# Three edits to a gated attention and feed-forward kernel: the engine that copies one weight chunk, the place of one score, and the order of the last gate and up tiles

## The chip, the cores and the metric

The kernel runs on one core of a Trainium2 chip. The metric is the device time of one execution in microseconds (us), taken as the median of repeated runs. Before the change it is 1260.15 us over three runs, which lie between 1259.91 and 1260.15 us.

Five engines of the core work side by side, each through its own instructions in order, and meet at semaphores. TensorE (PE; its weight loads are a row of their own, PEld) multiplies matrices into PSUM. VectorE (DVE) and ScalarE (ACT) do elementwise work and empty PSUM. GpSimd (POOL) does elementwise work on SBUF and issues some DMAs. SyncE (SP) issues the other DMAs.

## The reference

All inputs are float32. There are 2048 tokens of width 448, 16 heads of width 28, and a hidden width of 1792.

```python
def reference(A_x, A_wqkv, A_wo, B_x, B_W_gate, B_W_up, B_W_down, gate_w):
    x = A_x
    g = sigmoid((x * gate_w).sum(-1, keepdims=True))
    # a: attention with 16 heads
    q, k, v = split(x @ wqkv)
    p = softmax(q @ k.T * 28 ** -0.5)
    a = (p @ v) @ wo
    # b: gated feed-forward
    gate = x @ W_gate
    gate = gate * (gate > 0)
    b = (gate * (x @ W_up)) @ W_down
    return g * a + (1 - g) * b
```

## The kernel before

**Split numbers.** Matmuls run on rounded float32 (`F32R`). To keep the precision, an operand is held as a high part (a copy rounded to `F32R`) and a low part (the value minus its high part). A product of two split operands is a list of eleven matmuls (`TERMS`, L68), ordered by the chunk of 128 rows that they need (`BY_CHUNK`, L71). `act_high` (L129) makes a high part on ACT, `dve_high` (L132) on DVE; `low` (L135) makes a low part on DVE, `pool_low` (L138) on POOL. Chunks 0, 1 and 2 of a weight have low parts of their own (places 3, 4, 5); the fourth chunk has 64 rows, which stand twice in place 6, the upper half as high parts and the lower half as low parts.

**Opening.** `split_first` (L270) splits the first group of 224 weight columns, chunk by chunk (`weights(c)`), and the first 512 tokens (`tokens(c)`), in four groups: weights 0 with tokens 0, weights 1 with tokens 1, weights 2 with weights 3, tokens 2 with tokens 3. In `weights(c)` ACT makes every high part; DVE makes the low part of chunk 0, POOL those of chunks 1, 2 and 3. In `tokens(c)` ACT makes the high and DVE the low part. The first projection, `qk(0, 0, BY_CHUNK)` (L415, matmuls at L352), follows the chunks as they come.

**Rounds.** Projections of queries, keys and values follow, with scores and row maxima mixed in. Then a list of rounds (`ROUNDS`, L63) runs the attention and, beside it, 50 of the 56 gate and up tiles. The order of a round is written out by hand as a string, one letter for each TensorE step: `s` one score matmul (L217), whose exponential ACT takes (L219) out of PSUM banks 0 and 1 in turn; `S` the same in another bank; `m` a row-maximum matmul (L191); `x` one gate or up matmul (L526); `l` sends the last projection to DRAM (an ACT and a DVE instruction and a POOL DMA); `u`, `U`, `h` handle the tiles' splits and ends. `FIRST` (L48) is the first round.

**The end.** From L817 on, the kernel works through a list `todo`. `done` is 50, so gate and up tiles 50 to 55 are left. `gate_up(i)` (L754) first issues the split of tile i+1 (`split_f`, L502: three ACT copies, then DVE low parts: two of 128x384 and two of 64x128, tile `wg`, two buffers) and the fetch of tile i+3 (SP), then 22 matmuls of its own tile, then `relu` (ACT) and `spill_h` (L544): DVE multiplies into `h`, and a POOL DMA writes `h` to DRAM. `down(i)` (L802) is 12 matmuls (L789) with the hidden tile `hh` and the down weights `WD`. Ahead of each `down(i)` the loop at L845 issues `fetch_d(i + 4)` (SP DMAs of `wdr` and `hr`) and `split_d(i + 2)` (L776): DVE copies the high part of `WD`, POOL makes its low part, ACT and DVE split `hh`. `split_wo(c)` (L709) does the same for chunk c of the output weights (a DVE copy into `WO`, then a POOL low part). `normalise(15)` (L584) scales the last head on DVE and writes it with four POOL DMAs. `fetch_o(0)` (L718) reads it back with three SP DMAs into the buffer that the raw output weights had. `split_o(0, c)` (L725) splits it in two halves: ACT high parts, POOL low parts of 128x1024 (tile `on`). `wout(0, 0)` (L739) is the first tile of the output projection: 11 matmuls (L744), of which the first seven read high parts and the last four read low parts of chunks 0, 1, 2, 3. Chunks 2 and 3 are in the second half.

Before the change the list runs: tile 50, tile 51, down 0, tile 52, down 1, tile 53, down 2, tile 54, down 3, tile 55, down 4, `wout(0, 0)`, down 5. The `split_wo` steps stand ahead of down 0, tile 52, down 1 and tile 53, `normalise(15)` ahead of down 1, `fetch_o(0)` ahead of down 2, and both halves of `split_o(0)` ahead of tile 55.

Of the kernel before, what the change touches and what calls it, by code (L numbers as in the profile page):

```python
# [26 lines left out]
NF = F // P  # L27
NB = 4
# [16 lines left out]

FIRST = ("ssssssssssssssssmmmmssuxxxxsxmlxsxsxmSxsxsxmSxsxUsxmxsxsxmxsxsxmxsxsxmxsxsxmxsxsxmxsxsxmxsxsxmxsxsxm"  # L48
         "xsxhh")

ONE = ("mSxMxsmSmsxxsMxmsmSxsMxmsmxsMSxsmsmxSMsxmsmSMsxmsxmSMssxmSmxsMsmxNsmxxsMmsxxsmxMxxmsmxsxMsmxsxmMsxms"
# [10 lines left out]

ROUNDS = [(FIRST, 4)] + [(TWO, 4), (THREE, 4), (ONE, 4)] * 7 + [(LATE, 6), (FINAL, 6)]  # L63
NP = 11
# [14 lines left out]
def gated_mix_kernel(ctx, tc, x, wq, wo, wgu, wd, out):  # L79
# [49 lines left out]
    def act_high(dst, src):  # L129
        nc.scalar.activation(dst, src, AF.Copy)  # L130
# [4 lines left out]
    def low(dst, src, high):  # L135
        nc.vector.tensor_tensor(dst, src, f32(high), op=OP.subtract)  # L136
# [99 lines left out]
    with tc.tile_pool(name="qkv", bufs=1) as pa:  # L236
# [33 lines left out]
        def split_first(wr, xr):  # L270

            r = wr.rearrange("p c (a j d) -> p c a j d", a=2, j=4)
            w = W[:, :, :2 * GD].rearrange("p c (j a d) -> p c a j d", a=2, j=4)

            def weights(c):
                act_high(w[:, c if c < 3 else 6], r[:, c])
                yield

                take = pool_low if c else low
                if c < 3:  # L280
                    take(w[:, 3 + c], r[:, c], w[:, c])
                else:
                    take(w[64:, 6], r[64:, 3], w[64:, 6])
                yield

            def tokens(c):
                part = xr[c // 2][2][:, c % 2:c % 2 + 1]
                act_high(X[0][0][:, c:c + 1], part)
                yield
                low(X[0][1][:, c:c + 1], part, X[0][0][:, c:c + 1])  # L290
                yield

            for group in ((weights(0), tokens(0)), (weights(1), tokens(1)), (weights(2), weights(3)),
                          (tokens(2), tokens(3))):
                for _ in range(2):
                    for part in group:
                        next(part)
# [194 lines left out]
    done = sum(n for _, n in ROUNDS) // 2  # L492
# [125 lines left out]
    for r, (order, nu) in enumerate(ROUNDS):  # L618
        ni = order.lower().count("s") // NB
        late = order in (LATE, FINAL)  # L620
        todo = list(range(nxt, nxt + nu))
# [10 lines left out]
        for o in order:  # L632
            if o in "sS":
                i, j = i0 + ns // NB, ns % NB
# [14 lines left out]
            elif o == "x":  # L649
                i, half, k = passes.pop(0)  # L650
# [3 lines left out]
                if k == NT - 1:  # L654
                    i, half, ps = units.pop()
# [161 lines left out]
    todo = [(gate_up, done), (row_sums, H - 1), (gate_up, done + 1)]  # L817
    for i in range(NB * NF):
        todo.append((down, i))
        if done + 2 + i < NB * NF:  # L820
            todo.append((gate_up, done + 2 + i))

    def before(i, *new):
        n = todo.index((down, i))
# [66 lines left out]
```

## Time and profile before

| | |
|---|---|
| median of 3 runs | 1260.15 us (1259.91 to 1260.15) |
| time of the profiled execution | 1259.94 us |
| its span, first to last instruction | 1258.2 us |
| TensorE matmul busy | 1252.8 us, 6687 matmuls |
| VectorE busy | 854.8 us, 1363 instructions |
| ScalarE busy | 748.4 us, 1424 instructions |
| GpSimd busy | 374.3 us, 569 instructions |
| granted TensorE clock, mean over the span | 1.0 |

A timeline row gives the start in us, the length in us, the engine, the line of the kernel, the operation, the tiles as written<-read, their shapes, and how many instructions in a row were merged into it. In square brackets stands the idle time of the engine ahead of the row and what ended it. Instructions of one engine overlap a little at their ends. The matmuls' lengths are modelled: they are pipelined, so the distance from one matmul's start to the next is the better measure, and that is what the text uses. The 1.74 us by which the profiled execution's time exceeds its span lie outside the first and last instruction.

### The profile page before, as it was taken

The page shows a single profiled execution, that of the slowest core. Times are in us where ns is not written, and L with a number is a line of the kernel's source. Part 1 is how long each engine was busy: PE and PEld are TensorE (multiplying, and loading weights), DVE is VectorE, ACT ScalarE, POOL GpSimd, SP SyncE. Part 2 cuts the span into 40 slices and gives each one's busy share as a digit, 9 for nine tenths or more (in the row PEclk, how much of TensorE's full clock was granted, in tenths as well). Part 3 has the DMA queues.
Part 4 walks back from the last instruction along what each step waited for, and adds up shares of the span by engine and source line. Part 5 has one row for each costly group of instructions (what it writes and reads, how often), then busy time and mean ns, then how long its engine had stood idle before and what let it go on. Part 6 is the DMA issues. An engine that isn't in the chain of part 4 may idle for free.

```text
span 1258.2 us, 18270 instructions
## 1 busy us (share of the span) xinstructions
PE 1252.8 (100%) x6687; PEld 919.1 (73%) x6687; DVE 854.8 (68%) x1363; ACT 748.4 (59%) x1424; POOL 374.3 (30%) x569
## 2 busy tenths in 40 slices
PE   9999999999999999999999999999999999999998
PEld 6888866677666676666766667766667666899997
DVE  6599767687777797776977778877778224663342
ACT  6312767686666776666866667766677773312121
POOL 4222222312334123423133331134222444651020
PEclk9999999999999999999999999999999999999999
DMA  8955453144245314241544323142431226634432
GB/s 302 315 206 209 117 155 99 50 106 104 60 115 173 81 43 121 68 113 44 130 121 127 100 80 90 43 122 67 114 94 50 84 85 208 223 110 138 145 106 79
DMA packets 54113, 151.00 MB, mean 120 GB/s; under 512 B 10304, under 2 KB 17416, under 8 KB 49160
## 3 DMA queue, kind: packets, MB, share of 16 engines
q1 hardware_dynamic: 36632, 100.44, 29.2%
q0 software_dynamic: 16960, 48.94, 11.0%
q8 instruction: 52, 0.85, 0.3%
q10 hardware_dynamic: 432, 0.46, 0.1%
q14 instruction: 37, 0.30, 0.1%
HBM read 104.16 MB, written 46.03 MB: 119 GB/s over the span
## 4 chain that ended last, share of the span: by engine, by line
PE 99%; DMA 0%; SPq 0%; DVE 0%; ACT 0%; issue 0%
PE b L526 22%; PE b L191 19%; PE b L217 19%; PE b L560 18%; PE b L789 11%; PE b L352 5%; PE b L370 3%; PE b L744 3%; DMA xr<-x 0%; PE b L199 0%; SPq L304 0%; DVE X L136 0%; DVE y L795 0%; ACT X L130 0%; SPq L384 0%
## 5 line engine op out<-in xcount | busy, mean ns | idle before, releaser
L192 DVE TENSOR_REDUCE mx<-b 128x1 f32<-128x512 f32 x1024 | 646.5, 685 | 51.2 <-PE b L191 50.7
L219 ACT ACTIVATE P<-b 128x512 f32<-128x512 f32 x840 | 467.1, 599 | 160.8 <-PE b L217 139.0
L526 PE MATMUL b<-X,wg 128*128 128x512 f32 (+1 forms) x1232 | 415.3, 394 | 0.0
L191 PE MATMUL b<-K,Q 128*128 128x512 f32 x1024 | 389.6, 391 | 0.0
L217 PE MATMUL b<-Q,K 128*128 128x512 f32 x1024 | 389.3, 390 | 0.0
L526 PEld LDWEIGHTS b<-X,wg 128*128 128x128 f32 (+1 forms) x1232 | 220.2, 187 | 53.8 <-issue 9.3
L217 PEld LDWEIGHTS b<-Q,K 128*128 128x128 f32 x1024 | 192.3, 188 | 46.3 <-issue 6.7
L191 PEld LDWEIGHTS b<-K,Q 128*128 128x128 f32 x1024 | 192.4, 188 | 44.3 <-issue 5.9
L560 PE MATMUL b<-P,V 128*32 128x512 f32 x1680 | 188.2, 593 | 0.0
L548 POOL DMA_DIRECT2D h_d<-h x56 | 31.3, 558 | 405.4 <-DVE h L542 354.9
L139 POOL TENSOR_TENSOR wg<-wgr,wg 128x384 fp32r<-128x384 f32 x200 | 143.2, 731 | 10.4 <-DVE wg L133 2.0
L560 PEld LDWEIGHTS b<-P,V 128*32 128x32 f32 x1680 | 52.7, 110 | 120.0 <-issue 116.8
L789 PE MATMUL b<-WD,hh 128*128 128x448 f32 x672 | 138.5, 365 | 0.0
L219 ACT ACTIVATE V<-b 128x512 f32<-128x512 f32 x184 | 105.0, 599 | 48.8 <-PE b L217 42.3
L789 PEld LDWEIGHTS b<-WD,hh 128*128 128x128 f32 x672 | 126.2, 188 | 10.3
L130 ACT ACTIVATE hh<-hr 128x512 fp32r<-128x512 f32 x56 | 35.3, 631 | 124.7 <-PE b L789 120.2
L136 DVE TENSOR_TENSOR hh<-hr,hh 128x512 fp32r<-128x512 f32 x56 | 45.7, 815 | 66.4 <-ACT hh L130 66.3
L352 PE MATMUL b<-X,W 128*128 128x512 f32 x308 | 83.1, 393 | 0.1
L566 DVE TENSOR_TENSOR os<-b,os 128x512 f32<-128x512 f32 x16 | 11.1, 692 | 86.5 <-PE b L560 86.5
L352 PEld LDWEIGHTS b<-X,W 128*128 128x128 f32 x308 | 57.4, 188 | 14.5 <-DVE X L136 1.6
L130 ACT ACTIVATE wg<-wgr 128x384 fp32r<-128x384 f32 x156 | 62.2, 490 | 7.9 <-DMA wgr<-wgu 3.9
L575 POOL DMA_DIRECT2D l_d<-rs x16 | 8.9, 559 | 186.2 <-DVE rs L574 186.2
(74 smaller groups left out, 665.6 us busy)
## 6 DMA issues: line engine op xcount, KB each, us to landing
wgr<-wgu SPq DMA_DIRECT2D x55, 512.0 KB
K<-qk_d SPq DMA_DIRECT2D x64, 224.0 KB
Q<-qk_d SPq DMA_DIRECT2D x64, 224.0 KB
h_d<-h POOLq DMA_DIRECT2D x56, 256.0 KB, 2.7
hr<-h_d SPq DMA_DIRECT2D x56, 256.0 KB
qk_d<-st POOLq DMA_DIRECT2D x21, 512.0 KB, 4.2
x_d<-X POOLq DMA_DIRECT2D x6, 1024.0 KB, 5.4
X<-x_d SPq DMA_DIRECT2D x24, 256.0 KB
```

The source lines that it names most:

```text
L130: nc.scalar.activation(dst, src, AF.Copy)
L136: nc.vector.tensor_tensor(dst, src, f32(high), op=OP.subtract)
L139: nc.gpsimd.tensor_tensor(dst, src, f32(high), op=OP.subtract)
L191: nc.tensor.matmul(ps, Q[h][:, u * P:(u + 1) * P], K[h % 3][:, c * TB:(c + 1) * TB], start=True, stop=True)
L192: nc.vector.tensor_reduce(MX[h][:, 4 * u + c:4 * u + c + 1], ps, axis=AX.X, op=OP.max)
L217: nc.tensor.matmul(ps, K[h % 3][:, kt * P:(kt + 1) * P], Q[h][:, j * TB:(j + 1) * TB], start=True, stop=True)
L219: nc.scalar.activation(PT[i][:, j], ps, AF.Exp, scale=SCALE)
L352: nc.tensor.matmul(ps, W[:, a, c * P:(c + 1) * P], xf(tb, b), start=(n == 0), stop=(n == NT - 1))
L370: nc.tensor.matmul(ps[:, :VC], xf(tb, b)[:, t * P:(t + 1) * P], W[:, a, 2 * D:2 * D + VC], start=(n == 0), stop=(n == NT - 1))
L526: nc.tensor.matmul(ps, WS[i][rows, s, a], xf(i // NF, b)[rows], start=(n == 0), stop=(n == NT - 1))
L560: nc.tensor.matmul(po[32 * j:32 * j + 32], V[:, h // 4 % 2, i % NK, h % 4], p[:, j], start=(i == i0), stop=(i == i0 + ni - 1))
L789: nc.tensor.matmul(ACC[i // NF][t][:, :D], HH[i][:, a, t * P:(t + 1) * P], WD[:, f, b], start=(f == 0 and n == 0), stop=(f == NF - 1 and n ...
```

## The change

The high part of the fourth chunk of the first weights is copied by DVE and no longer by ACT. In the string of the first round, the pair `sx` behind `mlxs` becomes `xs`, so that one score is issued one gate or up matmul later. At the end, tiles are put on the list in pairs: down 0, tiles 52 and 53, down 1, down 2, tiles 54 and 55, down 3, down 4.

```diff
-FIRST = ("ssssssssssssssssmmmmssuxxxxsxmlxsxsxmSxsxsxmSxsxU...
+FIRST = ("ssssssssssssssssmmmmssuxxxxsxmlxsxxsmSxsxsxmSxsxU...
@@ split_first, weights(c)
-                act_high(w[:, c if c < 3 else 6], r[:, c])
+                (act_high if c < 3 else dve_high)(w[:, c if c < 3 else 6], r[:, c])
@@ the list of the end
     for i in range(NB * NF):
         todo.append((down, i))
-        if done + 2 + i < NB * NF:
-            todo.append((gate_up, done + 2 + i))
+
+        if i % 2 == 0:
+            todo += [(gate_up, k) for k in (done + 2 + i, done + 3 + i) if k < NB * NF]
```

The steps that hang on places of the list move with it. `split_wo` for chunk 3 now comes ahead of chunk 2, since tile 53 now comes ahead of down 1. `normalise(15)`, the split for down 3 and all that is issued ahead of down 1 come behind tile 53 on DVE, ACT, POOL and SP. On POOL the low parts of `WO` chunks 0 and 1 and of the down weights 2 keep their place ahead of tile 52's `h`. The splits of the down weights 5 and of hidden tile 5, issued ahead of down 3, and both halves of `split_o(0)` behind it, come behind tile 55: on POOL the order becomes the `h` writes of tiles 54 and 55, the low part of `WD` 5, then the two low parts of `on`. The matmuls themselves are the same on both sides.

More of the change, by code (lines that the diff above doesn't have):

```diff
@@ L42 @@
 LEAD = 24
-FIRST = ("ssssssssssssssssmmmmssuxxxxsxmlxsxsxmSxsxsxmSxsxUsxmxsxsxmxsxsxmxsxsxmxsxsxmxsxsxmxsxsxmxsxsxmxsxsxm"
+FIRST = ("ssssssssssssssssmmmmssuxxxxsxmlxsxxsmSxsxsxmSxsxUsxmxsxsxmxsxsxmxsxsxmxsxsxmxsxsxmxsxsxmxsxsxmxsxsxm"
          "xsxhh")
```

## The prediction

> **What bounds the kernel now.** I read the page first, then the chain of waits, then the timeline of each stretch that the edits touch. The page and the chain:
>
> ```profile
> span 1258.2 us, 18270 instructions
> PE 99%; DMA 0%; SPq 0%; DVE 0%; ACT 0%; issue 0%
> ```
>
> TensorE is the bound all the way. The edits change no matmul, so they can only gain where TensorE waits today, and lose where they make it wait. First the timeline of PE at the end, where the list is reordered; L526 is a gate and up tile, L789 a down, L744 a `wout`:
>
> ```profile
> 1064.34 5.21 PE L526 MATMUL b<-X,wg 128*128 128x512 f32 x22
> 1069.38 2.59 PE L789 MATMUL b<-WD,hh 128*128 128x448 f32 x12
> 1071.82 5.20 PE L526 MATMUL b<-X,wg 128*128 128x512 f32 x22
> 1076.86 2.59 PE L789 MATMUL b<-WD,hh 128*128 128x448 f32 x12
> ...
> 1086.76 5.21 PE L526 MATMUL b<-X,wg 128*128 128x512 f32 x22
> 1091.80 2.60 PE L789 MATMUL b<-WD,hh 128*128 128x448 f32 x12
> 1094.24 2.39 PE L744 MATMUL b<-WO,on 128*128 128x448 f32 x11
> ```
>
> From start to start a tile takes 5.04 us (1071.82 to 1076.86: 0.229 a matmul) and a down 2.43 to 2.44 (eleven matmuls of 448 columns at 0.203 make 2.23). There is no room between them: nothing to gain here. The tiles at 1064.34, 1071.82 and 1086.76 are 52, 53 and 55.
>
> **The pair 52 and 53.** Tile 53 moves ahead of down 1, so it comes 2.43 us sooner: at 1069.38. Its first matmul reads a high part, its second a low part of the `wg` tile that DVE makes. The timelines of DVE and POOL show when (the same rows as merged in another answer stand third):
>
> ```profile
> 1052.60 0.55 DVE L136 TENSOR_TENSOR wg<-wgr,wg 128x384 fp32r<-128x384 f32 x1
> ```
> ```profile
> 1066.46 0.38 DVE L133 CAST WO<-wor 128x448 fp32r<-128x448 f32 x1
> 1066.76 4.60 DVE L136 TENSOR_TENSOR wg<-wgr,wg 128x384 fp32r<-128x384 f32 x1
> ```
> ```profile
> 1066.76 5.59 DVE L136 TENSOR_TENSOR wg<-wgr,wg 128x384 fp32r<-128x384 f32 x4
> ```
> ```profile
> 1067.54 1.17 POOL L139 TENSOR_TENSOR WO<-wor,WO 128x448 fp32r<-128x448 f32 x1
> 1068.65 1.17 POOL L139 TENSOR_TENSOR WD<-wdr,WD 128x448 fp32r<-128x448 f32 x1
> 1069.76 1.17 POOL L139 TENSOR_TENSOR WO<-wor,WO 128x448 fp32r<-128x448 f32 x1
> ```
>
> A DVE low part of this shape takes 0.55 us; this one takes 4.60 and ends at 1071.36, which is 0.43 after the third of three POOL low parts in a row (1069.76 + 1.17 = 1070.93). So DVE stood still while POOL worked. Today that is hidden by down 1: tile 53 needs the part from 1071.82 + 0.23 = 1072.05 on, 0.7 us after it is there. After the change it is needed at 1069.38 + 0.23 = 1069.61. Nothing that DVE or POOL does up to there is moved: the same instructions stand in the same order ahead of it, tile 52 and down 0 keep their times, and ScalarE's copies for tile 53 are ahead of it too. So TensorE waits 1071.36 - 1069.61 = 1.75, with some 0.04 for the semaphore 1.79 us. The other three low parts end at 1072.35 (1066.76 + 5.59); the 64-row ones are wanted only by the tenth matmul, about 1073.3, and hide.
>
> A wait also costs a restart, since the weights are not loaded ahead. Its price is to be read where the moved score stands today, in the timelines of PE and of its weight loads:
>
> ```profile
> 146.23 0.39 PE L526 MATMUL b<-X,wg 128*128 128x512 f32 x1
> 146.46 0.50 PE L217 MATMUL b<-Q,K 128*128 128x512 f32 x1
> 146.80 0.40 PE L526 MATMUL b<-X,wg 128*128 128x512 f32 x1
> ```
> ```profile
> 146.46 0.19 PEld L217 LDWEIGHTS b<-Q,K 128*128 128x128 f32 x1 [0.26 <-ACT P L219]
> ```
>
> The score waited for an exponential to free its bank; the next matmul came 0.34 us behind it and not 0.23: 0.11 for a restart. Tile 53 therefore costs 1.79 + 0.11 = **1.90 us**.
>
> **The skill's rule on the port.** The Trainium skill, "SBUF — State Buffer", section "Who interferes with whom", says that a VectorE instruction with two SBUF inputs and a GpSimd instruction that reads SBUF exclude each other, and that the one that issued first has the port pair for its whole instruction. The exclusion agrees with the 4.60; the order does not, since DVE's row starts at 1066.76 and POOL's at 1067.54. By the rule the part would have been ready at 1066.84 + 0.55 = 1067.39 and the wait would not be; the third rival has that case worked out from the rows alone.
>
> **The pair 54 and 55.** Today's `normalise` on DVE and its DMAs on POOL:
>
> ```profile
> 1072.99 0.68 DVE L586 TENSOR_TENSOR os<-os,rb 128x512 f32<-128x512 f32 x1
> ```
> ```profile
> 1074.09 2.19 POOL L588 DMA_DIRECT2D o_d<-os  x4
> ```
>
> Down 1 and down 2 stand ahead of it (4.87 us), and then tile 55 follows 54 at once. POOL now has `h` 53, four `o_d` DMAs, `WO` 2, `WD` 3 and `WD` 4 in one run. From tile 53's end (today 1076.86, then 1069.38 + 5.04 + 1.90 = 1076.32) I count: `h` done 0.95 later (0.26 after the next group's first matmul, then 0.69, as in the row at 1092.06 below), `normalise` 0.6, 0.3 until a DMA starts behind DVE (1092.75 to 1093.05 below), the DMAs 2.2, three low parts at 1.11: 1083.7. If DVE's parts for tile 55 wait for all of that they come by 1084.8; tile 55 wants its first low part at 1076.32 + 4.87 + 5.04 + 0.23 = 1086.5. Covered by 1.7 us, so nothing. ScalarE's copies for tile 55 wait for tile 53's buffer and for `hh` 4, which waits for down 1's end at 1078.75; 2 us of copies behind it are done by 1081.
>
> **What is late next: `wout(0, 0)`.** Both halves of `split_o(0)` and `WD` 5 fall behind tile 55. Today's rows, POOL, then DVE, then ACT:
>
> ```profile
> 1087.27 4.76 POOL L139 TENSOR_TENSOR on<-or,on 128x1024 fp32r<-128x1024 f32 x2
> 1093.05 0.56 POOL L548 DMA_DIRECT2D h_d<-h  x1 [1.02 <-DVE WD L133]
> 1093.63 1.16 POOL L139 TENSOR_TENSOR WD<-wdr,WD 128x448 fp32r<-128x448 f32 x1
> ```
> ```profile
> 1092.06 0.69 DVE L542 TENSOR_TENSOR h<-b,rl 128x512 f32<-128x512 f32 x1 [5.88 <-PE b L526]
> ```
> ```profile
> 1084.97 1.06 ACT L130 ACTIVATE on<-or 128x1024 fp32r<-128x1024 f32 x1 [1.82 <-DMA or<-o_d]
> 1086.94 1.06 ACT L130 ACTIVATE on<-or 128x1024 fp32r<-128x1024 f32 x1 [0.91 <-DMA or<-o_d]
> ```
>
> Today the `on` parts run beside tile 55 and are done at 1092.03, 2.2 us ahead of `wout` at 1094.24. Let E be the end of tile 55 (today 1091.80). POOL's low part of `WD` starts 1.83 behind E (1093.63), because `h` 55 and its DMA come first, and ends at E + 2.99. Then come the two `on` parts at 2.38 each: E + 7.7. TensorE does down 3 and down 4 (4.87), then nine matmuls of `wout` at 0.203 (1.82), and wants chunk 2 at E + 6.7. That is 1.05 us of waiting, with the restart 1.16, if VectorE stays out. It does not: DVE has the next `WD` copy and `hh` low part queued. Where both engines meet later in today's run, on POOL and DVE:
>
> ```profile
> 1103.90 2.54 POOL L139 TENSOR_TENSOR on<-or,on 128x1024 fp32r<-128x1024 f32 x1
> 1106.39 1.60 POOL L139 TENSOR_TENSOR WD<-wdr,WD 128x448 fp32r<-128x448 f32 x1
> ```
> ```profile
> 1102.83 1.35 DVE L133 CAST WD<-wdr 128x448 fp32r<-128x448 f32 x1
> 1104.42 2.56 DVE L136 TENSOR_TENSOR hh<-hr,hh 128x512 fp32r<-128x512 f32 x1 [0.24 <-ACT hh L130]
> ```
>
> The copy got in ahead of `on`, which took 2.54 and not 2.38, and the `hh` part ahead of the next POOL part, which took 1.60 and not 1.16: 0.60 together. I take this, since it is the same sequence of instructions: 1.16 + 0.60 = **1.76 us**, with 1.16 as the other end. The high parts of `on` are no later bound: `normalise` moves by 4.2 us, so the two ACT rows come to about 1089.2 and 1091.1 (SP's reads wait for `o_d` and for `WO` 2's low part, the last reader of their buffer, at the same time), and POOL wants them at E + 3.0, about 1094.3. The fetches of `wdr` and `hr` for downs 6 and 7 are queued on SP behind these reads and move as much; they are wanted behind `wout(0, 0)` and land before. Behind `wout(0, 0)` all runs as today, later by the sum.
>
> **The score.** Its bank came free just ahead of 146.46 (0.26 us of idle weight loads). One place later its weights are due at 146.46, ahead of a matmul at 146.69, so it waits for nothing and the restart goes: -0.11. Should the next scores wait in its place, 0.
>
> **The opening.** ACT, DVE, POOL and weight loads of today:
>
> ```profile
> 6.22 0.66 ACT L130 ACTIVATE W<-V 128x224 fp32r<-128x224 f32 x2
> 6.93 1.33 ACT L130 ACTIVATE X<-xr 128x512 fp32r<-128x512 f32 x2
> ```
> ```profile
> 6.35 0.69 DVE L136 TENSOR_TENSOR X<-xr,X 128x512 fp32r<-128x512 f32 x1 [0.30 <-ACT X L130]
> 7.59 1.68 DVE L136 TENSOR_TENSOR X<-xr,X 128x512 fp32r<-128x512 f32 x2 [0.55 <-ACT X L130]
> ```
> ```profile
> 6.68 0.89 POOL L139 TENSOR_TENSOR W<-V,W 128x224 fp32r<-128x224 f32 x1 [0.19 <-ACT W L130]
> 7.64 1.08 POOL L139 TENSOR_TENSOR W<-V,W 64x224 fp32r<-64x224 f32 x1
> ```
> ```profile
> 9.33 0.30 PEld L352 LDWEIGHTS b<-X,W 128*128 128x128 f32 x2 [0.36 <-DVE X L136]
> ```
>
> ACT is idle from 6.88 to 6.93 ahead of the tokens of chunk 2, so it waits for their data, and taking the copy of 0.38 away starts nothing sooner; at best, had the data been there, 0.33. The copy falls into DVE's idle 0.55 between 7.04 and 7.59, and POOL's part of chunk 3 cannot start before 7.57 anyway. If DVE then holds the port through both token parts, POOL's part and the last matmuls come up to 0.5 later. The last release is a token part at 9.33, as now. I take 0, with -0.3 and +0.5 as ends.
>
> **Sum.** 1.90 + 1.76 - 0.11 + 0 = 3.55 us on the profiled execution's 1259.94: 1263.5. That execution lies 0.2 below the median of 1260.15; I predict 1263.4.
>
> **The rivals.** (1) Both waits come, but VectorE gets no turn between POOL's parts: 1.90 + 1.16 - 0.11, 1262.9. (2) The opening or tile 55 adds a wait: if POOL's run of 1083.7 ends over 1.7 us later, each us is added; about 1264.5. Nothing in the rows is that late. (3) Not slower by more than the bound: VectorE gets the port at 1066.84 with tile 53's first low part and is done at 1067.39, from which point on the wait of 1.90 is gone; 1.16 to 1.76 of `wout` and -0.11 stay: 1261.0 to 1261.6. Against it stands the 4.60 itself, with the same instructions ahead of it; for it, that the port is granted by fractions of a microsecond. (4) Neither wait comes, since each engine has run ahead: 1259.8. Against it stands POOL's order, which puts `on` behind `h` 55.
>
> **How the numbers follow.** A measurement of this kernel can tell about 0.2% (2.5 us) from no change, so the line is 1262.7. Forecast 0.58, (1) 0.18, (2) 0.05, (3) 0.12, (4) 0.07, in which 0.01 is a gain of over 0.2%. Slower is the forecast, (2) and most of (1): 0.76; within is (3), most of (4), and a little of (1): 0.23. The range goes from (3) at 1261.0 to the forecast with the opening's 0.5 and a little more of `wout`: 1264.3.
>
> **What would show it.** Right: in the changed profile PE waits some 1.8 us for DVE `wg` right after the first matmul of tile 53, with the long DVE row still there, and 1 to 1.7 us for POOL `on` inside `wout(0, 0)`; the weight load of the moved score waits for nothing; the last wait of the opening stays near 9.33. Wrong: no long DVE row, or tile 53's matmuls in one piece; the `on` parts done ahead of the tenth matmul; a wait in tile 55.

## The result and the profile after

Over twelve runs each, the changed kernel takes 1263.03 us (1261.34 to 1265.32) and the kernel before 1260.15 us (1259.91 to 1260.61): a ratio of 1.0023, with a 95% interval of 1.0015 to 1.0031. It is slower by 2.9 us, 0.4 under the forecast. The runs of the changed kernel spread over 4 us, those of before over 0.7; the profiled execution of the changed kernel is the slowest of its twelve, at 1265.32 us, 5.38 over that of before. The head of the page and its chain of waits:

```profile
span 1263.5 us, 18272 instructions
PE 94%; DMA 3%; POOL 1%; SPq 1%; DVE 0%; issue 0%; ACT 0%; DVEq 0%; POOLq 0%
```

TensorE no longer carries 99% of the chain: GpSimd now stands on it with 1%, and DMAs, to which the last paragraphs of this section come, with 3%. The timeline of PE over the end, against the rows that the prediction shows of before:

```profile
1065.81 5.42 PE L526 MATMUL b<-X,wg 128*128 128x512 f32 x23
1073.84 5.07 PE L526 MATMUL b<-X,wg 128*128 128x512 f32 x21 [2.61 <-DVE wg L136]
1078.74 5.04 PE L789 MATMUL b<-WD,hh 128*128 128x448 f32 x24
1083.62 10.14 PE L526 MATMUL b<-X,wg 128*128 128x512 f32 x44
1093.60 5.03 PE L789 MATMUL b<-WD,hh 128*128 128x448 f32 x24
1098.47 1.99 PE L744 MATMUL b<-WO,on 128*128 128x448 f32 x9
1101.33 0.67 PE L744 MATMUL b<-WO,on 128*128 128x448 f32 x2 [0.87 <-POOL on L139]
1101.83 2.60 PE L789 MATMUL b<-WD,hh 128*128 128x448 f32 x12
```

A reader should see two breaks. The 44 matmuls of tiles 52 and 53 come as 23 and 21: after tile 53's first matmul TensorE stands, and VectorE's `wg` part releases it. Tiles 54 and 55 come in one piece, 44 matmuls in 9.98 us (1083.62 to 1093.60). Then `wout(0, 0)` breaks behind its ninth matmul, ahead of the low part of chunk 2. The waits of the weight loads between 1060 and 1110 us, which are all that this stretch has:

```profile
PEld b L526 <- DVE wg L136: 3.0, 1, 3.0
PEld b L744 <- POOL on L139: 1.3, 1, 1.3
```

**Where the 5.4 us came from.** Tile 52 starts 1.47 later than before (1065.81 against 1064.34). From there to the start of `wout(0, 0)` it is 32.66 us and not 29.90: 2.76 more. `wout(0, 0)` takes 3.36 (1098.47 to 1101.83), where eleven matmuls at 0.203 take 2.23: 1.13 more. Together 5.36.

**Tile 53.** VectorE's queue up to tile 53's first part, in the timeline of DVE:

```profile
1068.18 1.64 DVE L136 TENSOR_TENSOR hh<-hr,hh 128x512 fp32r<-128x512 f32 x1
1069.74 1.55 DVE L133 CAST WO<-wor 128x448 fp32r<-128x448 f32 x1
1071.21 2.57 DVE L136 TENSOR_TENSOR wg<-wgr,wg 128x384 fp32r<-128x384 f32 x1
```

And GpSimd beside it, in the timeline of POOL:

```profile
1067.63 2.22 POOL L582 DMA_DIRECT2D rb<-l_d  x4
1069.87 1.17 POOL L139 TENSOR_TENSOR WO<-wor,WO 128x448 fp32r<-128x448 f32 x1
1070.97 1.31 POOL L139 TENSOR_TENSOR WD<-wdr,WD 128x448 fp32r<-128x448 f32 x1
1072.25 1.12 POOL L139 TENSOR_TENSOR WO<-wor,WO 128x448 fp32r<-128x448 f32 x1
```

The part ends at 1073.78, that is 7.97 behind tile 52's start. In before it was 7.02 (1071.36 less 1064.34). The prediction's wait is there, and 0.95 longer. GpSimd is late by as much: its third low part ends 7.56 behind tile 52's start and not 6.59. The timeline of ACT has the cause, in the first split of a hidden tile at the end:

```profile
1061.96 0.63 ACT L130 ACTIVATE hh<-hr 128x512 fp32r<-128x512 f32 x1 [5.27 <-DMA hr<-h_d]
```

It waited for the hidden tile to be fetched from DRAM. The same row of before:

```profile
1059.79 0.63 ACT L130 ACTIVATE hh<-hr 128x512 fp32r<-128x512 f32 x1 [4.57 <-DMA hr<-h_d]
```

That is 4.55 ahead of tile 52's start; in the changed kernel it is 3.85 ahead, 0.70 later against TensorE. VectorE's low part waits for this copy, and `h` 51 and all else up to tile 53 is queued behind that, on VectorE and by its results on GpSimd. So a fetch from DRAM, a dozen VectorE instructions ahead, sets part of the wait.

**`wout(0, 0)`.** VectorE and GpSimd in their timelines, DVE first:

```profile
1095.36 6.17 DVE L133 CAST WD<-wdr 128x448 fp32r<-128x448 f32 x1
```
```profile
1094.85 0.55 POOL L548 DMA_DIRECT2D h_d<-h  x1 [4.43 <-DVE WD L133]
1095.41 1.17 POOL L139 TENSOR_TENSOR WD<-wdr,WD 128x448 fp32r<-128x448 f32 x1
1096.52 4.75 POOL L139 TENSOR_TENSOR on<-or,on 128x1024 fp32r<-128x1024 f32 x2
```

A copy of 0.38 us took 6.17: VectorE got no turn through three GpSimd parts. For GpSimd that was the better case: its `on` parts took 2.38 each and were done at 1101.27, which is 7.67 behind the end of tile 55 (1093.60). On TensorE only the output projection waited for them.

**The 1.47 ahead of tile 52.** The weight loads near 55 us, and the row-maximum matmuls on the page (at the end of the line the idle time of TensorE ahead of them, and what ended it):

```profile
55.75 0.19 PEld L191 LDWEIGHTS b<-K,Q 128*128 128x128 f32 x1 [1.64 <-issue]
```
```profile
L191 PE MATMUL b<-K,Q 128*128 128x512 f32 x1024 | 389.7, 391 | 1.2 <-DMA Q<-qk_d 1.2
```

This wait has no counterpart in before, whose page has 0.0 there: a row-maximum matmul waited for keys and queries to be read back from DRAM. (The expectations below call it the wait near 54 us, where it begins.) A second profile of the changed kernel, below, lacks it, so the change does not make it come each time; whether the change makes it more frequent is open. The opening's last release comes at 9.16, 0.17 sooner than in before.

### The profile page after: what moved, and what is told of

It is laid out like the page before. It is cut to its first block, busy times and chain, and to the rows that moved or that the text cites. A ratio compares the mean times of both kernels' runs of the same rounds, so it can differ in the third digit from the quotient of the medians.

```text
span 1263.5 us, 18272 instructions
## 1 busy us (share of the span) xinstructions
PE 1253.4 (99%) x6687; PEld 918.7 (73%) x6687; DVE 859.5 (68%) x1364; ACT 747.5 (59%) x1423; POOL 375.5 (30%) x569
## 4 chain that ended last, share of the span: by engine, by line
PE 94%; DMA 3%; POOL 1%; SPq 1%; DVE 0%; issue 0%; ACT 0%; DVEq 0%; POOLq 0%
PE b L526 22%; PE b L191 19%; PE b L217 19%; PE b L560 18%; PE b L789 10%; PE b L744 3%; PE b L352 3%; PE b L370 2%; DMA xr<-x 1%; DMA Q<-qk_d 1%; DMA qk_d<-K 0%; DMA wr<-wq 0%; POOL on L139 0%; PE b L199 0%; SPq L180 0%
```

## The experiments

**The theory**: the loss is two waits made by the new list alone. Tile 53 waits because GpSimd's three low parts in a row hold VectorE off, and `wout(0, 0)` waits because `on` stands behind `h` 55 and `WD` 5 on GpSimd. The copy and the score are nothing. **The rivals**: one of the other edits has a share (the wait at 55 us came with them); pairing costs something by itself, apart from these two waits; or the waits stay when what is said to cause them is taken away.

### The three edits, each alone

The kernel before with the edit of the list only:

```diff
-        if done + 2 + i < NB * NF:
-            todo.append((gate_up, done + 2 + i))
+        if i % 2 == 0:
+            todo += [(gate_up, k) for k in (done + 2 + i, done + 3 + i) if k < NB * NF]
```

> The kernel before with the new order of the last tiles alone. Theory (the pairs make TensorE wait for low parts that VectorE and GpSimd make late, and nothing else costs): all of the loss is here, 1262.5 to 1263.5 us, with a wait of 1.8 to 2.8 us behind the first matmul of tile 53 and 1.0 to 1.8 us inside wout(0, 0). Rival (the opening costs, as the 1.4 us wait at 54 us in the changed kernel's profile suggests): about 1261.5, and runs that scatter no more than those of before.

1262.75 us (1261.45 to 1264.01, 9 runs) against 1260.07: 1.0020 [1.0011, 1.0030]. The list alone makes the whole loss. But its profile shows tile 53 otherwise, in the timeline of PE and then of POOL:

```profile
1066.97 7.24 PE L526 MATMUL b<-X,wg 128*128 128x512 f32 x31
1074.38 3.25 PE L526 MATMUL b<-X,wg 128*128 128x512 f32 x13 [0.17 <-DVE wg L136]
1077.46 5.04 PE L789 MATMUL b<-WD,hh 128*128 128x448 f32 x24
```
```profile
1070.04 1.26 POOL L139 TENSOR_TENSOR WO<-wor,WO 128x448 fp32r<-128x448 f32 x1
1071.27 1.46 POOL L139 TENSOR_TENSOR WD<-wdr,WD 128x448 fp32r<-128x448 f32 x1
1072.70 1.47 POOL L139 TENSOR_TENSOR WO<-wor,WO 128x448 fp32r<-128x448 f32 x1
```

GpSimd's parts are stretched from 1.17 to 1.26, 1.46 and 1.47: here VectorE got in at each boundary, and its parts took 1.5 us each, as the timeline of DVE shows for the first two:

```profile
1070.22 2.94 DVE L136 TENSOR_TENSOR wg<-wgr,wg 128x384 fp32r<-128x384 f32 x2
```

Tile 53's second matmul was served in time, and the break is at its tenth (31 = 22 + 9), which wants the 64-row parts. From tile 52's start to down 1 it is 10.49 us. Two tiles with no wait between take 10.02 (the last experiment has the row), so tile 53 cost 0.47 here and, by the same measure, 12.93 - 10.02 = 2.91 in the profile above. The wait near 55 us is in this profile too, though the kernel has neither the new copy nor the new score. In this execution it counts for more than the two waits at the end: tile 52 starts 2.63 later than in before (1066.97 against 1064.34), out of the 4.07 between the two profiled executions. How much of the median's 2.7 it makes is not known.

The copy alone:

```diff
-                act_high(w[:, c if c < 3 else 6], r[:, c])
+                (act_high if c < 3 else dve_high)(w[:, c if c < 3 else 6], r[:, c])
```

> The kernel before with the copy of the fourth chunk on VectorE alone. Theory: 1260.0 to 1260.6, no wait near 54 us that the kernel before does not have. Rival (the opening costs): 1261.3 to 1261.7, with a wait of some 1.4 us near 54 us for the keys and queries that are read back.

1260.08 us (1259.73 to 1262.05, 11 runs) against 1260.07: 1.0001 [0.9992, 1.0010]. Its last release of the opening is at 9.34, where it was (9.33), and there is no wait near 55 us.

The score alone (behind `mlxsx` the pair `sx` is turned round: `sxmlxsxs` becomes `sxmlxsxx` and the score follows):

> The kernel before with the one score a place later alone. Theory: 1260.04, 0.11 less than before, which is below what can be told; in the profile the weight load of that score waits for nothing. Rival (a later score waits in its place): no difference in the time and the 0.11 found again a few matmuls on.

1259.91 us (1259.50 to 1261.10, 11 runs) against 1260.07: 0.9999 [0.9990, 1.0008]. In its profile the score's weights wait for nothing and the next matmul starts 0.23 behind the score's (146.48 and 146.71), so the restart is gone, as expected; a tenth of a microsecond can't be told in the times.

### Each pair alone

Tiles 52 and 53 paired, 54 and 55 as before:

```diff
-        if done + 2 + i < NB * NF:
+        if i == 0:
+            todo += [(gate_up, done + 2), (gate_up, done + 3)]
+        elif 1 < i and done + 2 + i < NB * NF:
             todo.append((gate_up, done + 2 + i))
```

> The kernel before with tiles 52 and 53 as a pair and tiles 54 and 55 one by one as before. Theory (two separate waits): only the wait behind tile 53's first matmul, 1.9 to 2.9 us, so 1262.0 to 1263.0, and wout(0, 0) without a wait, because the on parts stand ahead of tile 55. Rival (the wait in wout(0, 0) is carried over from the first pair, whose fetch of the attention output is late): a wait in wout(0, 0) too, in all over 1263.

1261.33 us (1260.08 to 1265.50, 11 runs) against 1260.07: 1.0012 [1.0003, 1.0021], less than expected. Its profile shows tile 53's wait nearly as the prediction works it out, in PE and then DVE:

```profile
1064.41 5.42 PE L526 MATMUL b<-X,wg 128*128 128x512 f32 x23
1071.32 5.06 PE L526 MATMUL b<-X,wg 128*128 128x512 f32 x21 [1.48 <-DVE wg L136]
1076.21 5.04 PE L789 MATMUL b<-WD,hh 128*128 128x448 f32 x24
```
```profile
1066.71 5.54 DVE L136 TENSOR_TENSOR wg<-wgr,wg 128x384 fp32r<-128x384 f32 x4
```

11.80 us from tile 52 to down 1, so 1.78 lost (1.90 was predicted), and `wout(0, 0)` runs in one piece: its wait belongs to the other pair. But runs of 1260.1 to 1260.3 stand beside it, in which tile 53 can hardly have waited.

Tiles 54 and 55 paired, 52 and 53 as before:

```diff
-        if done + 2 + i < NB * NF:
+        if i == 2:
+            todo += [(gate_up, done + 4), (gate_up, done + 5)]
+        elif i < 2:
             todo.append((gate_up, done + 2 + i))
```

> The kernel before with tiles 54 and 55 as a pair and tiles 52 and 53 one by one as before. Theory: only the wait in wout(0, 0), 1.0 to 1.2 us, the same in every run, since GpSimd runs the parts in one piece: 1261.1 to 1261.4 us with runs that scatter little. Rival (the wait near 54 us that two profiles with this pair show belongs to this pair): 1262.5 to 1263 with that wait of 1.4 to 1.9 us in the profile.

1264.26 us (1261.28 to 1264.73, 7 runs) against 1260.08: 1.0026 [1.0014, 1.0038]. The expectation is missed by 3 us. The timeline of PE:

```profile
1094.76 1.98 PE L744 MATMUL b<-WO,on 128*128 128x448 f32 x9
1097.60 0.68 PE L744 MATMUL b<-WO,on 128*128 128x448 f32 x2 [0.86 <-POOL on L139]
1098.12 2.64 PE L789 MATMUL b<-WD,hh 128*128 128x448 f32 x12
1100.60 2.44 PE L744 MATMUL b<-WO,on 128*128 128x448 f32 x11
```

The wait is the expected one: 3.36 - 2.23 = 1.13. The rest is new. From 1098.12 to 1100.60, twelve matmuls take 2.48 us, 206.7 ns each, and so it stays to the end; in the profile above, after the same wait, they take 2.44 (1101.83 to 1104.27), 203 ns. The 777 matmuls from there on at 4 ns make 3.1 us. Ahead of the restart the same execution has 203 ns as well. TensorE is never idle in it and its granted clock is 1.00.

The same kernel once more, to see whether that belongs to it:

> The kernel with the pair 54 and 55 alone once more. Theory (the wait in wout(0, 0) leaves TensorE in one of two rhythms, 202.7 or 206.7 ns a matmul of 448 columns, and keeps it to the end): either about 1261.2 or about 1264.3 in each run, few between, and in the profile one of the two distances throughout from the restart on. Rival (the first profile was a slow chip): all runs, the kernel before among them, are 2 to 3 us longer or none.

1262.01 us (1260.86 to 1265.02, 11 runs) against 1260.17: 1.0016 [1.0006, 1.0025], in two groups: six runs from 1260.86 to 1262.01, five from 1264.12 to 1265.02, and nothing between. The profile is one of the first group. Busy time of PE by windows, first of the run before, then of this one (window, its length, busy time with the number of matmul records, granted clock, DMA share, GB/s):

```profile
1150.00:1200.00 50.00, 50.00 (x243) 1.00 0.45 144
```
```profile
1150.00:1200.00 50.00, 50.00 (x249) 1.00 0.45 139
```

The same program, fully busy, at the same granted clock and much the same DMA load, does six matmuls fewer in these 50 us in the one execution than in the other. In the first group, whose middle is 1261.1, the pair costs 0.9 us, near the 1.1 that the theory gives it. The distance of the groups, about 3 us, is that of the slower rhythm, which was read in one profile only; that the other runs of the upper group are of this kind is argued, not shown.

### Taking the causes away

The changed kernel with the low parts of `WO` made by VectorE (`low` for `pool_low` in `split_wo`), so that of the three GpSimd parts beside tile 53's only that of `WD` is left:

> The changed kernel with the low parts of the output weights made by VectorE and not by GpSimd, so that four GpSimd parts leave the port there. Theory (tile 53 waits because VectorE is shut out by GpSimd): the long VectorE row of 2.6 to 4.6 us becomes at most 1.8, the wait behind tile 53's first matmul falls under 0.5 us, and the wait in wout(0, 0) stays: 1261.1 to 1261.9 and less scatter. Rival (VectorE is late by its own queue): VectorE has more work ahead of that part, so the wait grows by 1.2 us or more, over 1264.

1261.69 us (1261.19 to 1262.88, 11 runs) against 1260.08: 1.0013 [1.0004, 1.0022], as expected. In the timeline of PE, then of DVE:

```profile
1064.99 10.51 PE L526 MATMUL b<-X,wg 128*128 128x512 f32 x44
1075.33 5.04 PE L789 MATMUL b<-WD,hh 128*128 128x448 f32 x24
```
```profile
1069.82 1.55 DVE L136 TENSOR_TENSOR wg<-wgr,wg 128x384 fp32r<-128x384 f32 x4
```

The four parts take 1.55 us and not 5.5, tile 53 loses 0.32 (10.34 less 10.02), and the wait in `wout(0, 0)` stays (0.88 us of idle PE). The runs now lie within 1.7 us and not 4. That fits a tile 53 that spread them, but does not show it alone: the pair 54 and 55 without the other pair spreads over 4 us too.

The changed kernel with both halves of `split_o(0)` ahead of tile 55:

```diff
-            n = todo.index((down, i))
-            n -= todo[n - 1][0] is gate_up
+            n = todo.index((down, i) if tb else (gate_up, done + 5))
+            n -= tb and todo[n - 1][0] is gate_up
```

> The changed kernel with both halves of the split of the first attention output ahead of tile 55 and not behind it. Theory: no wait in wout(0, 0), the wait behind tile 53 stays with its scatter (0.3 to 2.8 us): 1260.3 to 1262.7, median near 1261.8. Rival (the output is read back too late in any order): a wait in wout(0, 0) or in tile 55 stays, and the time is that of the changed kernel, 1263.

1260.90 us (1260.12 to 1264.33, 11 runs, nine of them up to 1261.15) against 1260.08: 1.0009 [1.0000, 1.0019]. In its profile `on` is made beside tile 55 (1086.65 to 1091.42), and PE has no break in `wout(0, 0)`:

```profile
1094.67 2.39 PE L744 MATMUL b<-WO,on 128*128 128x448 f32 x11
```

That wait is GpSimd's order and nothing else. Tile 53 lost only 0.50 in this execution, and broke at its tenth matmul, as in the profile of the list alone. But the median is 0.9 under the 1261.8 expected: it fell by 2.1 us against the changed kernel, of which the wait accounts for 1.13. The rest has no cause in these profiles.

Both at once:

> The changed kernel with both of these repairs, so with all three edits and the pairs in place. Theory (the two waits are the whole loss): 1259.8 to 1260.4, the time of before, with runs within 1 us. Rival (something else of the change costs, as the wait near 54 us): 1261.3 or more.

1261.04 us (1260.01 to 1261.51, 11 runs) against 1260.08: 1.0005 [0.9997, 1.0014], 0.6 over what was expected. The reason is in DVE's queue: the low parts of `WO` that VectorE now makes stand ahead of tile 53's.

```profile
1068.71 0.63 DVE L136 TENSOR_TENSOR WO<-wor,WO 128x448 fp32r<-128x448 f32 x1
1069.25 1.55 DVE L136 TENSOR_TENSOR wg<-wgr,wg 128x384 fp32r<-128x384 f32 x4
```

The first `wg` part is there by about 1069.8, and tile 53 wants it at 1064.17 + 5.27 = 1069.44. The tile loses 0.61. This execution took 1260.22 us, though; what the longer runs lose beyond it no profile shows. Against the kernel with `WO` on VectorE alone the early `split_o(0)` gains 0.65 here (1261.69 to 1261.04), against 2.1 above, where the profiles give its wait 1.13 each time. The differences of medians don't add up to better than about 1 us.

The pair 54 and 55 alone, with `split_o(0)` ahead of tile 55:

> The kernel with the pair 54 and 55 alone, and the split of the first attention output ahead of tile 55. Theory (no wait in wout(0, 0), so no restart and no slow rhythm): 1260.0 to 1260.4, 202.7 ns a matmul to the end. Rival (the slow rhythm belongs to the order of the tiles): about 1263, with 206.7 ns in the profile.

1260.01 us (1259.75 to 1261.61, 11 runs) against 1260.17: 0.9997 [0.9988, 1.0006]. With its wait away the pair is free, and none of the eleven runs lies in the upper group. So pairing by itself costs nothing.

### The change once more, and a place for the wait to go

The changed kernel again, for the wait near 55 us and for tile 53:

> The changed kernel once more, for a second profile. Theory: again 1.1 us of waiting in wout(0, 0) and a wait between 0.3 and 2.8 us behind tile 53's first matmul; the wait near 54 us of its first profile comes with late landings in the opening, so it is there only if the second weights land at about 21 us and not at 19. Rival (the wait near 54 us belongs to the changed kernel): it is there again, 1.4 us or more, whatever lands when.

1263.10 us (1261.52 to 1266.34, 11 runs) against 1260.17: 1.0022 [1.0013, 1.0031], the first result over again. There is no wait near 55 us in this profile, though the second weights landed at 21.57 us and in the first at 21.50; what was expected from their landing falls. PE and then DVE (two parts merged):

```profile
1064.59 10.59 PE L526 MATMUL b<-X,wg 128*128 128x512 f32 x44
1075.01 5.04 PE L789 MATMUL b<-WD,hh 128*128 128x448 f32 x24
```
```profile
1066.92 4.63 DVE L136 TENSOR_TENSOR wg<-wgr,wg 128x384 fp32r<-128x384 f32 x2
```

The first part got the port ahead of GpSimd and took 0.55; the second then stood through all three of GpSimd's parts (to 1071.55). Tile 53 lost 0.40 here and 2.91 in the first profile of the same kernel.

Last, the changed kernel with `split_o(0)` early and all four `split_wo` behind tile 53:

```diff
-    for c, f in enumerate(((down, 0), (gate_up, done + 2), (down, 1), (gate_up, done + 3))):
+    for c, f in enumerate(((down, 1),) * 4):
```

> The changed kernel with all four steps of the output weights behind tile 53 (ahead of down 1) and the split of the first attention output ahead of tile 55; GpSimd makes the same parts as in the changed kernel. Theory: VectorE makes tile 53's low parts by 1067.5 on the clock of the kernel before, before GpSimd's next part, so no wait there: 1259.8 to 1260.4 with runs within 1 us. Rival (GpSimd's run of parts moves the wait to tile 55, the second rival of the prediction): a wait of 0.5 to 2 us behind tile 55's first matmul, 1260.6 to 1262.

1260.96 us (1260.44 to 1263.22, 11 runs) against 1260.17: 1.0003 [0.9995, 1.0012]. PE, DVE and POOL:

```profile
1064.51 10.19 PE L526 MATMUL b<-X,wg 128*128 128x512 f32 x44
1074.53 5.04 PE L789 MATMUL b<-WD,hh 128*128 128x448 f32 x24
1079.41 5.37 PE L526 MATMUL b<-X,wg 128*128 128x512 f32 x23
1085.37 5.09 PE L526 MATMUL b<-X,wg 128*128 128x512 f32 x21 [0.59 <-DVE wg L136]
```
```profile
1078.12 4.21 DVE L133 CAST WD<-wdr 128x448 fp32r<-128x448 f32 x1
```
```profile
1078.70 4.63 POOL L139 TENSOR_TENSOR WO<-wor,WO 128x448 fp32r<-128x448 f32 x4
```

Tile 53 is free (10.02 us from tile 52 to down 1), and the four `WO` parts, now in one run, hold a VectorE copy for 4.21 us a little later (to 1082.33, through the first three of them), ahead of tile 55's parts: tile 55 waits instead. The wait follows the run of GpSimd parts to wherever a tile comes soon behind it.

No version tried is measurably faster than the kernel before.

## Why the prediction was right

**The pair 52 and 53: the mechanism right, the size of 1.90 only one case.** The wait is there, behind the first matmul of tile 53, and moving GpSimd's `WO` parts to VectorE takes most of it away. By the measure above it is 2.91, 0.40, 0.47 and 1.78 in the four profiles of kernels that have this pair with the old splits and no more, 0.50 with `split_o(0)` moved. The prediction took VectorE's 4.60 from one execution as fixed. Two things move it: what VectorE is behind by (the late fetch of a hidden tile makes most of the 0.95 of the first profile), and at which of GpSimd's boundaries VectorE gets in. The third rival named the latter ("granted by fractions of a microsecond"), at a chance of 0.12, and in three of these five profiles VectorE did get a turn. What the rival missed is that some wait is left when the first part slips in: the parts behind it are held off instead, up to the 64-row ones, which the prediction put down as hidden.

The kernels without this pair have the same GpSimd parts in the same order, and their profiles show the same cases: tile 53's first part took 4.60 in before and 4.58 with the score alone, 0.54 with the copy alone, and with the pair 54 and 55 alone 4.58 in the first profile and 1.50, in turns, in the second of the same program. So the 1.90 rests on the case that one profile happened to hold. The medians' 2.9 less the 1.13 of `wout(0, 0)` leave 1.7, near it; but that remainder also holds whatever the runs have of the wait near 55 us and of the slower rhythm, and with `split_o(0)` early the same tile 53 leaves 0.8 in all. What tile 53 costs in the median is not shown.

**The port.** The exclusion of the Trainium skill ("SBUF — State Buffer", "Who interferes with whom") is borne out by the experiment with VectorE's `WO` parts. That the first to issue has the port agrees with the changed kernel's second profile (0.55) but not with the 1066.71 row of the pair 52 and 53 alone, which starts 0.78 ahead of GpSimd's first part (1067.49) and stood all the same. With the copy alone, a part with the same lead of 0.78 (1066.73 and 1067.51) took 0.54. So the lead that these rows show does not decide it.

**The pair 54 and 55.** Right: the pair was covered, and tile 55 never waited except where the `WO` parts were moved in front of it, by the mechanism of the second rival.

**`wout(0, 0)`: the place right, the size 1.76 wrong, 1.13 measured.** The step that failed is "It does not: DVE has the next `WD` copy and `hh` low part queued": they were queued, and got no turn in any profile that has this wait. The count without VectorE (GpSimd done 7.7 behind tile 55's end, a wait of 1.16) was measured as 7.67 and 1.13; the first rival's assumption holds. In the rows used to argue the turn, from 1103.90 on, VectorE did get in between GpSimd parts that follow each other just as closely; why there and not here is open.

**The score and the opening.** Right: the restart at 146.46 is gone and not to be seen in the times; the opening's last release lies between 9.12 and 9.59 in the seven profiles with the copy and between 9.04 and 9.45 in the seven without, so the 0 holds as far as single executions can tell.

**What was not foreseen.** That the loss would vary so much from run to run: the median of 2.9 lies between executions that lose 1.2 and 6. And that two neighbouring tiles take 9.98 to 10.03 us and not twice 5.04, a gain of up to 0.1 for each pair that the sum left out.

**The sum.** It came to 3.55 us, and the medians differ by 2.88: 0.67 too much, nearly all of it the 0.63 of `wout(0, 0)`. That the other terms fit so closely is luck, since tile 53 lost between 0.40 and 2.91 from one execution to the next. The last step of the forecast has the wrong sign: the profiled execution of before lies 0.2 under the median, so the sum on the median is 1260.15 + 3.55 = 1263.7 and not 1263.4. The first rival, VectorE without a turn, comes out at 1262.9, or at 1263.1 on the median; it is nearer to the measured 1263.03 than the forecast, and what it assumes is what the profiles show in `wout(0, 0)`.

**What stays open.** What decides at which boundary the port changes hands. What makes the wait near 55 us: it is in the profiles of the change and of its list edit (1.64 and 2.1 us of idle weight loads), in small in three others (0.7 or less), and missing in the second profile of the changed kernel, so it differs between executions of one program; whether the new list makes it more frequent is not known, and it can have a share in the median's 2.9. What sets the slower rhythm, and whether it also accounts for the changed kernel's longest runs, which no profile caught. It does not simply follow from the wait in `wout(0, 0)`: with `WO` on VectorE that wait is there, and none of the eleven runs exceeds 1262.88; and the kernel before, without any of these waits, has single runs of 1263.02 and 1264.01 among the 33 beside the last experiments.

## What to carry to other kernels

When a step is moved ahead of another, look at the engines that feed it as they stand at the new time: the work between was the cover for a VectorE part that a run of GpSimd parts held off. Where VectorE and GpSimd share a stretch, bound the VectorE part by the end of the whole run of GpSimd parts, expect anything between that and no delay, and put the wanted transfers and splits of the slow engine ahead of what can wait, as `on` ahead of `h` 55. A wait whose length hangs on such a race is worth a second profile before it is put down as one number.

## What the runs showed of the hardware

- **VectorE behind GpSimd.** With GpSimd's parts back to back, VectorE instructions of 0.38 and 0.55 us took 4.2 to 6.2 (6.17 and 4.60 along three parts, 4.21 along the first three of four), and in other executions of the same order they took turns, both sides stretched (GpSimd 1.17 to 1.47, VectorE 0.55 to 1.50).
- **VectorE behind GpSimd's DMA issues.** In the first profile an `hh` part beside four `rb` DMA issues took 1.64 and not 0.68, and ended with them (1069.82 and 1069.85). In the profiles of before and of the repeat, such parts beside the same issues took 0.68. So it happens, but not always.
- **Two rhythms of TensorE at the same granted clock.** After a restart the 448-column matmuls came every 206.7 ns to the end in one execution, and every 202.7 to 203 ns in the thirteen other profiles, each at a granted clock of 1.00 between 1150 and 1200 us and with no idle time there.
